# First batch of a fused attention and SoLU layer: P kept in float32 and turned by TensorE, with fewer TensorE turns of z

## The chip, the cores and the metric

One core of a Trainium2 chip runs the whole program. The metric is the device time of one execution in microseconds, as the median over several runs; the kernel before was run three times.

## What is computed

Two parts in a row. Attention with decay over 8 batches of 8 heads, sequence 576, head width 64:

```
scores = q k^T / 8 + (cum_q - cum_k), masked above the diagonal; cum = cumsum(log(clip(f, 1e-4, 1)))
P      = exp(scores - max) / (sum + 1e-9)
attn   = P v
```

Its output, 4608 tokens of 512, goes through one feed-forward layer:

```
h    = x w_in                       (512 -> 1024)
solu = h * softmax(h)
z    = (solu - mean) / sqrt(var + 1e-6) * g_ln
out  = z w_out                      (1024 -> 512)
```

Everything is float32 at the interface. Inside, most products are made from float16 halves: an operand is split into a high and a low half, and three products (high-high, low-high, high-low) stand for one.

## The kernel before, in words

**Attention.** Two heads make a pair, four pairs a batch, 32 pairs (p = 0 to 31) in all. A pair's 576 query rows lie in five tiles (i = 0 to 4): the first has 64 rows, the others 128; tile i needs 64 + 128 i key columns, so a tile's width is 64, 192, 320, 448 or 576. `score_products` makes the scores on TensorE in PSUM (the first 8 pairs in float32, the later ones from float16 halves). `scores` does the rest of the softmax: DVE adds the mask and takes the maximum (L839), ACT takes the exponential and its sum (L844), GpSimd prepares the divisor (L850), DVE inverts it (L851). For tiles 0 and 1 (`HOME`) the exponentials stay in PSUM, for tiles 2 to 4 they go to SBUF (`pt`). Then P is split: a cast to float16 with the division (`copied`, L500 on ACT for tiles 0 to 3, L502 on GpSimd for tile 4; table `P_HI`), and the rest as a low half by DVE (L866). `transposes` turns both halves by a DMA issued on SP (`turned_dma`, L509), one DMA for each tile, 160 in all. `values` multiplies by v, whose halves `split_v` has made (L782 on GpSimd, L783 on DVE): for each tile i there are i + 1 key blocks, 15 a pair, each with three float16 products for each of two heads, which run side by side in two column halves of the array (L888). ACT and DVE split the result into the layer's x (`x_h` L897, `x_l` L898).

**The layer.** 36 blocks of 128 tokens ("layers" 0 to 35 below). 24 products of 512 columns make h (L918 to L920) in one PSUM tile `hps`; DVE takes the maximum (L929), ACT the exponential (L932), DVE the weighted product (L936), ACT the squares (L946), GpSimd the statistics (L940 to L951). Then z is normalised and turned, with 24 products behind it (L988 to L990; the last layer has its own, L1001 to L1004). For layers `TURNED[0]` <= n < `TURNED[1]`, before 3 to 32, z is normalised by GpSimd (L956), split into halves by ACT (L500) and GpSimd (L960), and turned by one DMA. In the other six, GpSimd or DVE normalises z (L965), TensorE turns it (L976, eight turns of 128 columns), and ACT and DVE split it as they take it out of PSUM (L979, L980).

**Weights.** The inputs are stored as pairs of 32-bit words, from which ACT and DVE decode float32 values: ACT one word (L579), then the top bits of the other, either by ACT into PSUM in two halves (L593) with two DVE passes (L599), or, where `W_TOP` says GpSimd, in one pass of 1024 columns in SBUF and one DVE pass. Eight such blocks: four of W_in, four of W_out. ACT sums squares of W_out (L728) for its scale and of v (L680) for theirs.

**Order.** Every piece of work is recorded by `op(engine, ns, due, ...)`. `Plan.schedule` walks through time with the planner's costs `ns` and its own delays, and on each engine takes, of what can start, the piece with the smallest `due`. `due` is not the time given at the call but `RANK[seq]`, a table of some 3,700 numbers. The result is a fixed instruction order on each engine. Six PSUM banks (`ps`) are handed out by the plan. Where the plan leaves TensorE idle in its first 300 us, products of the identity with itself (fillers, L1112, 256 columns) are put into the order:

```
                for _ in range(many):
                    nc.tensor.matmul(dst[:, :256], blank[:, :P], blank, start=True, stop=True)
```

The first half (tiles 0 to 2) of all four pairs of batch 0 comes first, then the second half (tiles 3 and 4); layers 0 and 1 (tokens under 320) need the first half alone.

Of the kernel before, what the change touches and what calls it, by code (L numbers as in the profile page):

```python
# [1156 lines left out]
```

## Time and profile before

| | |
|---|---|
| median of 3 runs | 682.15 us (680.62 to 682.84) |
| profiled execution | 680.34 us, its span 678.6 us |
| TensorE busy | 648.1 us (95% of the span) |
| DVE, ACT, GpSimd busy | 567.1, 528.8, 374.4 us |
[...]

The busy time of TensorE counts fillers as it counts real products, and a product's duration includes its drain, in which the next one already runs; the pace of a run of products is read from the distance of their starts. "Idle before" in a row is the time that the engine stood idle ahead of the group, with what ended it.

### The profile page before, as it was taken

Reading aid. Unit: us, or ns where it says so; the run is one execution under the profiler, and the core shown is the slowest. Engines: PE = TensorE matmul, PEld = TensorE weight load, DVE = VectorE, ACT = ScalarE, POOL = GpSimd, SP = SyncE. Lnnn points to the kernel's source line nnn. Section 1 sums busy time; section 2 is a strip of 40 time slices with the busy share of each in tenths; the row PEclk is TensorE's granted clock in tenths of the full one; section 3 lists DMA queues with packets and bytes.
Section 4 is the critical chain, followed back from the end, with each engine's and each line's share of the span. In section 5 each row is a group of like instructions: output and inputs, shape, how many; then the busy total and the mean of one; then the engine's idle time right before and its main releaser. Section 6 shows DMA issues by size and latency. Waiting matters only on the chain. (4 is left out here: it accounts for less than half of the span.)

```text
span 678.6 us, 17916 instructions
## 1 busy us (share of the span) xinstructions
PE 648.1 (95%) x6573; PEld 355.4 (52%) x6573; DVE 567.1 (84%) x1672; ACT 528.8 (78%) x1320; POOL 374.4 (55%) x591
## 2 busy tenths in 40 slices
PE   6999999999998999999999999998999999899998
PEld 4667555555544445545454545454454555454545
DVE  6796999998997899999899879999999987766232
ACT  6999977799878977979887878978776787665423
POOL 3211364456557845767578746776576854454410
PEclk9999999999999999999999999999999999999999
DMA  8999579989989998999699799898864986487501
GB/s 338 329 237 312 102 126 168 226 167 145 182 135 234 176 196 146 204 201 213 136 219 223 126 199 176 151 192 208 155 118 88 194 136 122 92 156 145 116 1 62
DMA packets 284280, 116.21 MB, mean 171 GB/s; under 512 B 269856, under 2 KB 270304, under 8 KB 283168
## 3 DMA queue, kind: packets, MB, share of 16 engines
q1 hardware_dynamic: 284192, 115.07, 81.8%
q8 instruction: 51, 0.84, 0.5%
q14 instruction: 37, 0.30, 0.2%
HBM read 38.27 MB, written 9.66 MB: 71 GB/s over the span
## 5 line engine op out<-in xcount | busy, mean ns | idle before, releaser
L844 ACT ACTIVATE p<-p,nm 128x448 f32<-128x448 f32 (+2 forms) x192 | 126.9, 662 | 30.1 <-DVE nm L839 27.7
L850 POOL TENSOR_SCALAR sm<-sm 128x2 f32<-128x2 f32 (+1 forms) x128 | 39.6, 309 | 149.6 <-ACT p L844 104.9
L818 PE MATMUL ps<-qk 64*128 64x288 f16 (+9 forms) x1056 | 105.1, 305 | 11.2 <-DVE nm L839 4.2
L918 PE MATMUL hps<-wi_h,x_h 128*128 128x512 f16 x288 | 109.6, 381 | 4.9 <-DVE e L936 4.9
L920 PE MATMUL hps<-wi_h,x_l 128*128 128x512 f16 x288 | 109.1, 379 | 0.0
L919 PE MATMUL hps<-wi_l,x_h 128*128 128x512 f16 x288 | 109.1, 379 | 0.0
L866 DVE SCALAR_TENSOR_TENSOR wo_p<-p,ri,wo_p 128x576 f16<-128x576 f32 (+1 forms) x128 | 104.8, 845 | 3.6 <-POOL wo_p L502 2.1
L988 PE MATMUL ps<-wo_f,zz 128*128 128x512 f16 x280 | 106.7, 381 | 1.0 <-DVE nm L839 0.4
L990 PE MATMUL ps<-wo_f,zz 128*128 128x512 f16 x280 | 106.1, 379 | 0.0
L989 PE MATMUL ps<-wo_f,zz 128*128 128x512 f16 x280 | 106.1, 379 | 0.0
L888 PEld LDWEIGHTS <-v 128*64 128x64 f16 x2880 | 81.6, 110 | 31.8 <-issue 28.0
L888 PE MATMUL ps<-t_p,v 128*64 128x128 f16 (+1 forms) x2880 | 93.4, 219 | 4.4 <-DMA t_p<-p16s 1.3
L839 DVE CUSTOM_DVE_ANT_0 p<-ps,mask 128x448 f32<-128x448 f32 (+2 forms) x192 | 94.2, 513 | 2.9 <-PE ps L816 2.5
L960 POOL TENSOR_TENSOR z<-e,z 128x1024 f16<-128x1024 f32 x30 | 66.7, 2222 | 19.1 <-ACT z L500 18.5
L502 POOL TENSOR_SCALAR wo_p<-p,ri 128x576 f16<-128x576 f32 x64 | 54.7, 862 | 17.8 <-DVE ri L851 13.3
L929 DVE TENSOR_REDUCE st<-hps 128x1 f32<-128x1024 f32 x36 | 43.7, 1215 | 13.7 <-PE hps L920 13.4
L936 DVE SCALAR_TENSOR_TENSOR e<-hps,e 128x1024 f32<-128x1024 f32 x36 | 43.9, 1220 | 12.9 <-ACT e L932 12.8
L818 PEld LDWEIGHTS <-qk 64*128 64x128 f16 x864 | 32.9, 94 | 39.8 <-issue 26.9
L932 ACT ACTIVATE e<-hps,st,unscale 128x1024 f32<-128x1024 f32 x32 | 38.4, 1201 | 19.4 <-DVE st L930 18.1
L816 PE MATMUL ps<-crow,pick 64*128 64x448 bf16 (+1 forms) x360 | 52.4, 276 | 0.0
L866 DVE SCALAR_TENSOR_TENSOR p16s<-ps,ri,p16s 64x64 f16<-64x64 f32 (+1 forms) x128 | 38.9, 338 | 14.2 <-ACT p16s L500 13.9
L500 ACT ACTIVATE wo_p<-p,ri 128x448 f16<-128x448 f32 x64 | 40.0, 660 | 13.7 <-DVE ri L851 8.8
(178 smaller groups left out, 1305.8 us busy)
## 6 DMA issues: line engine op xcount, KB each, us to landing
raws<-in_qk_dram SPq DMA_DIRECT2D x24, 576.0 KB, 5.1
vraw<-in_v_dram SPq DMA_DIRECT2D x8, 1280.0 KB, 7.2
out_dram<-y SPq DMA_DIRECT2D x35, 256.0 KB, 2.8
qk<-in_qk_dram SPq DMA_DIRECT2D x8, 576.0 KB, 7.4
wo_raw<-in_w_in_dram SPq DMA_DIRECT2D x4, 1024.0 KB, 8.6
vraw<-in_w_out_dram SPq DMA_DIRECT2D x2, 1024.0 KB, 5.3
t_raw<-in_w_out_dram SPq DMA_DIRECT2D x2, 1024.0 KB, 6.2
t_p<-p16s SPq DMA_TRANSPOSE x96, 3.6
```

Of the source, the lines that this page charges most:

```text
L818: nc.tensor.matmul(dst, x[row(h), 0, q0:q0 + P], y[row(h), 1, cols], start=(n == 0), stop=False)
L839: op(DVE, R_NS[i] if n == 0 else 442, at[i][h] + STEPS[0], lambda i=i, h=h, n=n, a=a, e=e, x=x, m0=m0: nc.vector.tensor_tensor_reduce(home ...
L844: op(ACT, E_NS[i] + (28 if i in (2, 3) else 0), at[i][h] + STEPS[1], lambda i=i, h=h, x=x: nc.scalar.activation(home(i, h), home(i, h), AF ...
L866: op(DVE, L_NS[j], at[j][g] + STEPS[4], lambda j=j, g=g, nq=nq, h16=h16, l16=l16, r1=r1: nc.vector.scalar_tensor_tensor(l16(), home(j, g, ...
L888: nc.tensor.matmul(o[row(h), a:a + n], v16[m][:, x, 2 * j + h], t[:, y, i + j if h else i - j], start=(j == 0 and c == 0), stop=(j == i an ...
L918: nc.tensor.matmul(hps[:, sl], x_h, wi_h[:, c, sl], start=(c == 0), stop=False)
L919: nc.tensor.matmul(hps[:, sl], x_h, wi_l[:, c, sl], start=False, stop=False)
L920: nc.tensor.matmul(hps[:, sl], x_l, wi_h[:, c, sl], start=False, stop=(c == NCC - 1))
L960: op(Z_LO[n], {DVE: 1280, POOL: 2130}[Z_LO[n]], at, lambda: engine(Z_LO[n]).tensor_tensor(z16[:, :, 1], e2, z16[:, :, 0], ALU.subtract), [ ...
L988: nc.tensor.matmul(o, zz[:, a, 0, j], wo(0, k), start=(k == 0), stop=False)
L989: nc.tensor.matmul(o, zz[:, a, 0, j], wo(1, k), start=False, stop=False)
L990: nc.tensor.matmul(o, zz[:, a, 1, j], wo(0, k), start=False, stop=(k == NFC - 1))
```

## The change

- **P of the first batch** (pairs under `NFP * NPAIR` = 4) is not split. The exponentials of all five tiles go to SBUF (`banked` replaces `HOME`). GpSimd divides them in place, in float32 (`P_SCALE`, 10 instructions a pair). TensorE turns them in blocks of 128 columns, up to four to a PSUM bank (`pieces`; 25 blocks a pair); ACT (tiles 0 to 2) or DVE (tiles 3 and 4) copies them to SBUF (`T_COPY`, 9 copies a pair). The products with v are float32 on the raw v; v's scale moves to the pass that takes x out of PSUM. `split_v` is left out for these pairs.
- **W_out's top bits** are read by GpSimd (`W_TOP`), with one DVE pass instead of two.
- **z of layers 33 and 34** is turned by DMA too (`TURNED`).
- **`RANK`** is another table throughout.

```
+NFP = 1
+P_SCALE, T_COPY = (3, 3, 3, 3, 3), (1, 1, 1, 2, 2)
-W_TOP = (1, 1, 1, 1, 1, 1, 1, 1)
+W_TOP = (1, 1, 1, 1, 3, 3, 3, 3)
-TURNED = (3, 33)
+TURNED = (3, 35)
...
+        if p < NFP * NPAIR:
+            for j, g in each:
+                nq, w = q_n(j), 64 + P * j
+                copied(P_SCALE[j], {POOL: N_NS[j], ACT: 187 + 0.83 * w, DVE: 67 + 0.6 * w}, at[j][g] + STEPS[3], *[lambda j=j, g=g, nq=nq: home(j, g, nq)] * 2,
+                       [("ri", m, j), ("p", j)], [("p", j, g)], scale=ri[m][:nq, j, g:g + 1], by=1.0 / P_UP)
+            return
...
+                def turn(a=a, e=e, key=key):
+                    for s in range(a, e):
+                        nc.tensor.transpose(ps[plan.place[key]][:, (s - a) * nq:(s - a + 1) * nq], pt[i][:nq, s * P:s * P + P], ident[:nq, :nq])
...
+            if exact:
+                t = t.rearrange("p x s w -> p (x s w)").bitcast(F32).rearrange("p (s w) -> p s w", w=n)
+                for j in range(i + 1):
+                    for h in range(2):
+                        nc.tensor.matmul(o[row(h), a:a + n], vraw[b % 2][:, hp, 2 * j + h], t[:, i + j if h else i - j], start=(j == 0), stop=(j == i))
+                return
...
-        split_v(p, at + due["v"] + AT_P[p][1])
+        if p >= NFP * NPAIR:
+            split_v(p, at + due["v"] + AT_P[p][1])
```

How the order moves, at three places. Lines of the changed kernel are shifted: L500 and L502 become L507 and L509, L506 and L509 (DMAs) L513 and L516, L818 becomes L825, L844 L851, L888 L928, L897 L938, L918 L959, L1112 L1154.

ACT, before, up to the first `x_h` of the first batch (`p16s` are the halves of tiles 0 to 2, `p_63` the exponentials of tile 2, `ps` PSUM banks):

```order
L500 ACTIVATE p16s_81<-ps_145,ri_89 128x192
L844 ACTIVATE p_63,sm_93<-p_63,nm_85 128x320 x2
L500 ACTIVATE p16s_81<-ps_145,ri_89 64x64
L500 ACTIVATE p16s_81<-ps_143,ri_89 128x192
L844 ACTIVATE ps_147,sm_94<-ps_147,nm_86 128x64
L500 ACTIVATE p16s_81<-p_63,ri_89 128x320 x2
L844 ACTIVATE ps_146,sm_94<-ps_146,nm_86 128x64
L844 ACTIVATE ps_146,sm_94<-ps_146,nm_86 128x192
L844 ACTIVATE ps_147,sm_94<-ps_147,nm_86 128x192
L500 ACTIVATE p16s_81<-ps_143,ri_89 64x64
L897 ACTIVATE x_h<-ps_145 128x320
```

The same engine in the change, behind its first `x_h` and up to the second (`t_0_p`, `t_1_p` are the turned P):

```order
L938 ACTIVATE x_h<-ps_146,scale_117 128x320
L851 ACTIVATE p_63,sm_95<-p_63,nm_87 128x64
L851 ACTIVATE p_64,sm_95<-p_64,nm_87 128x192
L851 ACTIVATE p_63,sm_95<-p_63,nm_87 128x64
L507 ACTIVATE t_1_p<-ps_148 128x384
L851 ACTIVATE p_64,sm_95<-p_64,nm_87 128x192
L507 ACTIVATE wi_h<-z_104,scale_wi 128x1024
L851 ACTIVATE p_65,sm_95<-p_65,nm_87 128x320 x2
L507 ACTIVATE wi_h<-e_103,scale_wi 128x1024
L938 ACTIVATE x_h<-ps_146,scale_117 128x320
```

The casts of P are gone from ACT, copies of turned P stand between the exponentials, and all exponentials are in SBUF tiles.

TensorE, before, at a short run of fillers between two pairs' products with v:

```order
L888 LDWEIGHTS v_1_78
L888 MATMUL ps_145<-t_1_p,v_1_78 64x128
L1112 LDWEIGHTS ident
L1112 MATMUL hps<-ident 128x256
L1112 LDWEIGHTS ident
L1112 MATMUL hps<-ident 128x256
L888 LDWEIGHTS v_0_77
L888 MATMUL ps_144<-t_0_p,v_0_77 64x64
```

TensorE in the change, just ahead of the first layer's first product (L923 are float32 products with v, L898 turns of P, the float32 weight load being part of the instruction):

```order
L923 MATMUL ps_146<-t_1_p,vraw_76 64x128 x10
L898 MATMUL ps_148<-ident,p_66 128x128 x4
L898 MATMUL ps_150<-ident,p_66 128x128 x3
L1154 LDWEIGHTS ident
L1154 MATMUL ps_145<-ident 128x256
L1154 LDWEIGHTS ident
L1154 MATMUL ps_145<-ident 128x256
L898 MATMUL ps_145<-ident,p_67 128x128 x3
L898 MATMUL ps_146<-ident,p_67 128x128 x3
L959 LDWEIGHTS x_h
L959 MATMUL hps<-wi_h,x_h 128x512
```

In TensorE's whole order there are 363 fillers before and 130 in the change.

SP, the DMA queue, before, behind the loads of the inputs (`c_scratch` and `crow` are the prefix sums on their way through DRAM):

```order
L506 DMA c_scratch<-t_0_cc 32x1728
L509 DMA_TRANSPOSE t_0_p<-p16s_81 128x10x128
L509 DMA_TRANSPOSE t_0_p<-p16s_81 128x2x64
L509 DMA_TRANSPOSE t_0_p<-p16s_81 128x6x128
L509 DMA_TRANSPOSE t_1_p<-p16s_82 128x2x64
L509 DMA_TRANSPOSE t_1_p<-p16s_82 128x6x128
L506 DMA crow<-c_scratch 48x576 x2
L506 DMA c_scratch<-t_0_cc 32x1728
L509 DMA_TRANSPOSE t_1_p<-p16s_82 128x10x128
L506 DMA vraw_75<-in_w_out_dram 128x2048
L506 DMA t_0_raw<-in_w_out_dram 128x2048
```

And in the change:

```order
L513 DMA c_scratch<-t_0_cc 32x1728
L513 DMA crow<-c_scratch 48x576
L513 DMA c_scratch<-t_0_cc 32x1728
L513 DMA crow<-c_scratch 48x576 x3
L513 DMA t_0_raw<-in_w_out_dram 128x2048
L513 DMA vraw_77<-in_w_out_dram 128x2048
L513 DMA qk_0_70<-in_qk_dram 128x1152
L513 DMA t_0_raw<-in_w_out_dram 128x2048
```

The first batch's 20 turning DMAs are gone, and the loads of W_out stand directly behind the prefix sums.

## Rows read from the trace of the kernel before

**Rows 1.** Windows: length; busy us of PE, PEld, DVE, ACT, POOL; granted clock; DMA; GB/s.

```profile
20.00:77.00 57.00, 52.81 (x559) 39.71 (x555) 46.84 (x152) 55.41 (x136) 12.92 (x28) 1.00 0.89 244
100.00:120.00 20.00, 19.66 (x204) 10.74 (x204) 19.59 (x69) 16.25 (x51) 9.88 (x18) 1.00 0.90 164
```

**Rows 2.** Timeline, TensorE, at 77 us: start, us, engine, line, operation.

```profile
77.12 0.39 PE L918 MATMUL hps<-wi_h,x_h 128*128 128x512 f16 x1
```

**Rows 3.** Windows of line L1112 (fillers) alone.

```profile
0.00:77.00 77.00, 44.31 (x346) 33.58 (x346) 0.98 0.88 271
77.00:680.00 603.00, 2.55 (x17) 1.49 (x17) 1.00 0.82 158
```

**Rows 4.** Timeline, TensorE, at 20 us: a run of fillers.

```profile
20.28 3.01 PE L1112 MATMUL hps<-ident 128*128 128x256 bf16 x26
```

**Rows 5.** Timeline, TensorE, at 645 us: four turns of z.

```profile
645.24 0.60 PE L976 MATMUL ps<-ident,z 128*128 128x128 f32 x4
645.68 0.38 PE L988 MATMUL ps<-wo_f,zz 128*128 128x512 f16 x1
```

**Rows 6.** Chain of work that ended last: products with v of a whole pair.

```profile
524.45 2.56 PE ps L888 x90
```

**Rows 7.** Timeline, TensorE, at 18 us: float32 score products of two heads.

```profile
18.48 0.57 PE L818 MATMUL ps<-qk 64*128 64x192 f32 x4
18.89 0.41 PE L814 MATMUL ps<-t_cc,e 64*128 64x192 bf16 x6
19.14 0.80 PE L818 MATMUL ps<-qk 64*128 64x320 f32 x4
19.77 0.44 PE L814 MATMUL ps<-t_cc,e 64*128 64x320 bf16 x4
```

**Rows 8.** Timeline, layer 32's maximum and its turning DMA; then landing times of such DMAs.

```profile
625.16 1.22 DVE L929 TENSOR_REDUCE st<-hps 128x1 f32<-128x1024 f32 x1 [2.61 <-PE hps L920]
636.27 1.93 SPq L509 DMA_TRANSPOSE zz<-z  x1
DMA to landing us min/median/max: 4.2/4.4/6.0
```

**Rows 9.** Groups, ACT: busy us, mean ns of one, idle before and its releasers.

```profile
L500 ACT ACTIVATE wo_p<-p,ri 128x448 f16<-128x448 f32 x64 | 40.0, 660 | 13.7 <-DVE ri L851 8.8 <-issue 4.4 <-POOL unscale_(0, 1)_131 L708 0.5
L500 ACT ACTIVATE p16s<-p,ri 128x320 f16<-128x320 f32 x64 | 33.9, 556 | 3.5 <-DVE ri L851 3.0 <-ACT p L844 0.3
L500 ACT ACTIVATE p16s<-ps,ri 128x192 f16<-128x192 f32 x64 | 25.5, 411 | 2.3 <-DVE ri L851 1.4 <-ACT p L844 0.6
L500 ACT ACTIVATE p16s<-ps,ri 64x64 f16<-64x64 f32 x64 | 18.8, 304 | 0.4 <-DVE p16s L866 0.2
L593 ACT ACTIVATE ps<-t_raw 128x512 int32<-128x512 uint8 x4 | 2.5, 626 | 0.0
```

**Rows 10.** Groups, DVE (the first and last hold two shapes each).

```profile
L866 DVE SCALAR_TENSOR_TENSOR wo_p<-p,ri,wo_p 128x576 f16<-128x576 f32 (+1 forms) x128 | 104.8, 845 | 3.6 <-POOL wo_p L502 2.1
L866 DVE SCALAR_TENSOR_TENSOR p16s<-p,ri,p16s 128x320 f16<-128x320 f32 x64 | 40.8, 658 | 2.8 <-ACT p16s L500 2.5
L980 DVE TENSOR_TENSOR zz<-ps,zz 128x512 f16<-128x512 f32 x12 | 8.1, 682 | 14.8 <-ACT zz L979 14.7
L866 DVE SCALAR_TENSOR_TENSOR p16s<-ps,ri,p16s 64x64 f16<-64x64 f32 (+1 forms) x128 | 38.9, 338 | 14.2 <-ACT p16s L500 13.9
```

**Rows 11.** Groups, GpSimd; the third is from the timeline at 622 us.

```profile
L502 POOL TENSOR_SCALAR wo_p<-p,ri 128x576 f16<-128x576 f32 x64 | 54.7, 862 | 17.8 <-DVE ri L851 13.3 <-DVE wo_f L744 3.2
L956 POOL TENSOR_SCALAR e<-e,st 128x1024 f32<-128x1024 f32 x30 | 43.2, 1441 | 2.7
622.66 0.74 POOL L502 TENSOR_SCALAR wo_p<-p,ri 128x576 f16<-128x576 f32 x1 [0.30 <-DVE ri L851]
```

**Rows 12.** Windows at the first lower clock.

```profile
8.00:14.00 6.00, 1.29 (x17) 0.85 (x16) 5.46 (x10) 5.21 (x10) 0.75 (x2) 0.96 1.00 419
14.00:16.00 2.00, 2.00 (x16) 1.57 (x16) 2.00 (x5) 1.50 (x2) 1.51 (x4) 0.50 1.06 446
```

More of the change, by code (lines that the diff above doesn't have):

```diff
@@ L27, with banked @@
 BIG = 3.0e38
+def banked(p, i):
+    return HOME[i] and p >= NFP * NPAIR
 def q_lo(i):
@@ L408, in buf @@
         return held[tag][1]
-    pt = [None if HOME[i] else sb(f"p_{i}", (2 * i + 1) * P) for i in range(NQ)]
+    pt = [sb(f"p_{i}", (2 * i + 1) * P) for i in range(NQ)]
     mask = sb("mask", S + P, dtype=BF16)
@@ L494, in engine, with copied @@
         return {DVE: nc.vector, POOL: nc.gpsimd}[e]
-    def copied(eng, ns, due, out_, in_, reads, writes, scale=1.0, clear=(), port=True):
+    def copied(eng, ns, due, out_, in_, reads, writes, scale=1.0, clear=(), port=True, by=1.0):
         def fn():
@@ L501, in fn @@
             else:
-                (nc.vector if eng == DVE else nc.gpsimd).tensor_scalar(now(out_), now(in_), scale, 1.0, ALU.mult, ALU.mult)
+                (nc.vector if eng == DVE else nc.gpsimd).tensor_scalar(now(out_), now(in_), scale, by, ALU.mult, ALU.mult)
         op(eng, ns[eng], due, fn, reads, writes, clear=clear, port=port and eng == DVE)
@@ L830, in home @@
             w = 64 + P * i
-            return bank(p, i, h)[:nq, :w] if HOME[i] else pt[i][:nq, h * w:(h + 1) * w]
+            return bank(p, i, h)[:nq, :w] if banked(p, i) else pt[i][:nq, h * w:(h + 1) * w]
         def token(i, h):
-            return ("sb", *score_keys(p, i, h)[0]) if HOME[i] else ("p", i, h)
+            return ("sb", *score_keys(p, i, h)[0]) if banked(p, i) else ("p", i, h)
         for i, h in each:
@@ L840, in scores @@
                     home(i, h)[:, a:e], bank(p, i, h, n)[:, :e - a], mask[:, m0 + a:m0 + e], -0.125 / (QK if p >= NAT * NPAIR else 1.0), x if n else BIG, ALU.add, ALU.min, accum_out=x),
-                   [score_keys(p, i, h)[n], ("mask",)], [token(i, h), ("nm", m, i, h)], clear=[] if HOME[i] else [("p", i)])
+                   [score_keys(p, i, h)[n], ("mask",)], [token(i, h), ("nm", m, i, h)], clear=[] if banked(p, i) else [("p", i)])
         for i, h in each:
             x = nm[m][:, i, h:h + 1]
-            op(ACT, E_NS[i] + (28 if i in (2, 3) else 0), at[i][h] + STEPS[1], lambda i=i, h=h, x=x: nc.scalar.activation(
+            op(ACT, E_NS[i] + (0 if banked(p, i) or i == 4 else 28), at[i][h] + STEPS[1], lambda i=i, h=h, x=x: nc.scalar.activation(
                 home(i, h), home(i, h), AF.Exp, bias=x, scale=-1.0, accum_out=sm[m][:, i, h:h + 1]),
-               [*(score_keys(p, i, h) if HOME[i] else []), ("nm", m, i, h), ("table",)], [token(i, h), ("sm", m, i, h)])
+               [*(score_keys(p, i, h) if banked(p, i) else []), ("nm", m, i, h), ("table",)], [token(i, h), ("sm", m, i, h)])
         i = group[-1]
@@ L855, in scores @@
             h16 = lambda w=w, j=j, g=g, nq=nq: p16(p, j, 0)[:nq, g * w:(g + 1) * w]
-            reads = [("ri", m, j), *score_keys(p, j, g), token(j, g)] if HOME[j] else [("ri", m, j), ("p", j, g), ("p", j)]
-            prior = [("w32", c) for c in (2 * n2, 2 * n2 + 1)] + [("w32", "s", k) for k in range(4 * n2, 4 * n2 + 4)] if p < 2 and j > 2 else []
-            copied(P_HI[j], {POOL: N_NS[j], ACT: (158 if HOME[j] else 187) + 0.83 * w, DVE: 67 + 1.05 * w}, at[j][g] + STEPS[3], h16, lambda j=j, g=g, nq=nq: home(j, g, nq),
-                   reads, [("p16", n2, j, g)], scale=r1, clear=prior, port=not HOME[j])
+            reads = [("ri", m, j), *score_keys(p, j, g), token(j, g)] if banked(p, j) else [("ri", m, j), ("p", j, g), ("p", j)]
+            prior = [("w32", c) for c in (2 * n2, 2 * n2 + 1)] + [("w32", "s", k) for k in range(4 * n2, 4 * n2 + 4)] if p - NFP * NPAIR < 2 and j > 2 else []
+            copied(P_HI[j], {POOL: N_NS[j], ACT: (158 if banked(p, j) else 187) + 0.83 * w, DVE: 67 + 1.05 * w}, at[j][g] + STEPS[3], h16, lambda j=j, g=g, nq=nq: home(j, g, nq),
+                   reads, [("p16", n2, j, g)], scale=r1, clear=prior, port=not banked(p, j))
         for j, g in each:
@@ L863, in scores, with pieces @@
             h16, l16 = (lambda n=n, w=w, j=j, g=g, nq=nq: p16(p, j, n)[:nq, g * w:(g + 1) * w] for n in range(2))
-            reads = [("ri", m, j), *score_keys(p, j, g), token(j, g)] if HOME[j] else [("ri", m, j), ("p", j, g), ("p", j)]
-            prior = [("w32", c) for c in (2 * n2, 2 * n2 + 1)] + [("w32", "s", k) for k in range(4 * n2, 4 * n2 + 4)] if p < 2 and j > 2 else []
+            reads = [("ri", m, j), *score_keys(p, j, g), token(j, g)] if banked(p, j) else [("ri", m, j), ("p", j, g), ("p", j)]
+            prior = [("w32", c) for c in (2 * n2, 2 * n2 + 1)] + [("w32", "s", k) for k in range(4 * n2, 4 * n2 + 4)] if p - NFP * NPAIR < 2 and j > 2 else []
             op(DVE, L_NS[j], at[j][g] + STEPS[4], lambda j=j, g=g, nq=nq, h16=h16, l16=l16, r1=r1: nc.vector.scalar_tensor_tensor(l16(), home(j, g, nq), r1, h16(), ALU.mult, ALU.subtract),
-               [*reads, ("p16", n2, j, g)], [("p16l", n2, j, g)], port=not HOME[j], clear=prior)
+               [*reads, ("p16", n2, j, g)], [("p16l", n2, j, g)], port=not banked(p, j), clear=prior)
+    def pieces(i):
+        n = 2 * i + 1
+        k = -(-n // 4)
+        return [(n * c // k, n * (c + 1) // k) for c in range(k)]
     def transposes(p, i, at):
@@ L871, in transposes @@
         to = [("t1raw",)] if i > 2 and p == 0 else []
+        if p < NFP * NPAIR:
+            t = lambda: turned_p(p, i).rearrange("p x s w -> p (x s w)").bitcast(F32)
+            for c, (a, e) in enumerate(pieces(i)):
+                key = ("s", "pt", p, i, c)
+                def turn(a=a, e=e, key=key):
+                    for s in range(a, e):
+                        nc.tensor.transpose(ps[plan.place[key]][:, (s - a) * nq:(s - a + 1) * nq], pt[i][:nq, s * P:s * P + P], ident[:nq, :nq])
+                op(PE, (e - a) * TRANSPOSE, at + 0.1 * c, turn, [("p", i), ("p", i, 0), ("p", i, 1), ("const",)], [key], take=key, form=TURNS)
+                w = (e - a) * nq
+                copied(T_COPY[i], {ACT: 75 + 0.83 * w, DVE: 72 + 1.05 * w}, at + 0.1 * c + 0.5, lambda a=a, e=e: t()[:, a * nq:e * nq], lambda w=w, key=key: ps[plan.place[key]][:, :w],
+                       [key], [("pt", m * (i < 3), i, c)], clear=[("pt", m * (i < 3), i), *to], port=False)
+            return
         turned_dma(at, lambda: turned_p(p, i).rearrange("p x s w -> p (x s) w"), lambda: p16(p, i)[:nq], nq // 16 * 2 * (2 * i + 1),
@@ L880, in values @@
         tiles = ((0, 1, 2), (3, 4))[half]
+        exact = p < NFP * NPAIR
         def product(i):
@@ L884, in product @@
             a, n = q_lo(i) - 320 * half, q_n(i)
+            if exact:
[3 more added lines that the diff above has]
+                        nc.tensor.matmul(o[row(h), a:a + n], vraw[b % 2][:, hp, 2 * j + h], t[:, i + j if h else i - j], start=(j == 0), stop=(j == i))
+                return
             for j in range(i + 1):
@@ L891, in values @@
         for i in tiles:
-            ns = (6 if i else 3.6) * (i + 1) * 30
-            op(PE, ns, at + 0.2 * (i - tiles[0]), lambda i=i: product(i), [("pt", p % 2 * (i < 3), i), ("v16", m), ("v16l", m)], [key],
+            ns = (6 if i else 3.6) * (i + 1) * (40 if exact else 30)
+            reads = [("vr", b % 2, hp), *(("pt", p % 2 * (i < 3), i, c) for c in range(len(pieces(i))))] if exact else [("v16", m), ("v16l", m)]
+            op(PE, ns, at + 0.2 * (i - tiles[0]), lambda i=i: product(i), [("pt", p % 2 * (i < 3), i), *reads], [key],
                take=key if i == tiles[0] else None, clear=[xk], form=HALVES)
-        up = 1.0 / P_UP
+        up, uk = (scales[b][:, 1, 0:1], [("scale", b, 0)]) if exact else (1.0 / P_UP, [])
         xo = [t[:, hp, x0:x0 + w] for t in x16]
-        op(ACT, 68 + 0.83 * w, at + XSTEP[0], lambda: nc.scalar.activation(xo[0], ps[plan.place[key]][:, :w], AF.Copy, scale=up), [key], [xk])
+        op(ACT, 68 + 0.83 * w, at + XSTEP[0], lambda: nc.scalar.activation(xo[0], ps[plan.place[key]][:, :w], AF.Copy, scale=up), [key, *uk], [xk])
         op(DVE, 72 + 1.05 * w, at + XSTEP[1], lambda: nc.vector.scalar_tensor_tensor(
-            xo[1], ps[plan.place[key]][:, :w], up, xo[0], ALU.mult, ALU.subtract), [key, xk], [(*xk, "l")], clear=[xk])
+            xo[1], ps[plan.place[key]][:, :w], up, xo[0], ALU.mult, ALU.subtract), [key, xk, *uk], [(*xk, "l")], clear=[xk])
     def layer(n, at):
```

290 rows, old and new, of the table RANK are left out of this document.

## The prediction

> **What bounds the kernel now.** I read the windows first. Between 20 and 77 us ACT is busy 55.4 of 57 us, DVE 46.8, GpSimd 12.9; between 100 and 120 us TensorE (19.66 of 20) and DVE (19.59) are the full ones [rows 1]. So there are two stages: a start that ends at 77.12 us, when the first layer's first product runs [rows 2], and a rest that is set by TensorE. TensorE's 52.8 busy us in the start mislead: the windows of line L1112 alone show 346 of its 363 filler products before 77 us and 17 after [rows 3]. A filler computes nothing; 26 in a row take 3.01 us, the last one's drain of 0.27 included, so one is (3.01 - 0.27)/25 = 0.109 us [rows 4] and 346 are 37.8 us. Of the first 77.1 us only 39.3 hold real products and waits. The start is set by ACT, and TensorE is padded while it waits.
>
> **The change part by part, on TensorE's own line.** The fillers are instructions of the program; each costs its time whatever is late, so they belong in the sum. The order of the change holds 130: 111 before the first layer's first product, 19 behind it.
>
> 1. Fillers: 363 - 130 = 233 fewer, 233 x 0.109 = -25.5 us (235 fewer before the first layer, 2 more behind).
> 2. P of the first batch is turned by TensorE: 25 blocks a pair, 100 for four pairs. Four such turns of z take 645.68 - 645.24 = 0.44 us [rows 5], 0.109 each: +10.9 us, 49 of them before the first layer, 51 behind.
> 3. P times v: a pair has 15 steps of two products side by side. Before, a step was three f16 passes: 90 products, 45 passes of two, in 2.56 us [rows 6], 0.057 a pass, 0.171 a step. Now it is one float32 step of 128 columns, which no row shows. The nearest are float32 score products, side by side too: 192 columns took 18.89 - 18.48 = 0.41 us, 320 took 0.63 [rows 7]; on the line through them 128 columns take 0.30, the upper bound. The lower bound is four times the f16 pace, 0.227. Each score product there comes behind other work and its surplus over four passes is about the same at 192 and 320 columns (0.07 and 0.06), as an entry cost; steps in a row should pay it seldom, so I take 0.25. 60 steps x (0.25 - 0.171) = +4.7 us, between +3.4 and +7.7.
> 4. z of layers 33 and 34 goes by DMA: 16 turns fewer, -1.7 us. Their wait: in layer 32 the maximum starts at 625.16, the turning DMA is issued at 636.27 and lands 4.2 to 6.0 us later [rows 8], 15.3 to 17.1 us. Behind layer 34's last input product the order holds 81 products of 512 columns from other layers; at twice a filler's 256 columns, 0.218 us each, they are 17.7 us: covered with little to spare, 0 to +1 us; I take 0.
>
> Sum: -25.5 + 10.9 + 4.7 - 1.7 = -11.6 us, if TensorE's unfilled waits stay as they are. Up to the first layer: -235 x 0.109 + 49 x 0.109 + 24 steps (the three small tiles of four pairs) x 0.079 = -18.4, so the first layer starts near 58.7 us; behind it +6.8 come back (51 turns, 36 steps, 2 fillers, less 1.7).
>
> **Can the engine that sets the start follow?** ACT's rows in front of the fourth x_h, for which the first layer waits, are the test. The order shows what leaves: 24 casts of P at 0.304, 0.411 and 0.556 us (8 of each, 10.2 us) and 2 at 0.660 (1.3); 8 reads of W_out's top bits at 0.626 (5.0) [rows 9]; and, put behind it, 13 wider passes (3 casts, 5 squares and 2 decodings of W_out, 3 squares of v), each of 512 columns or more and so at least the 0.660 of a 448-column cast: 8.6 us or more. What comes: 16 copies out of PSUM, 4 of 64 columns, 4 of 256, 8 of 384. By the casts' rows 64 columns are 0.30 and 384 lie between 0.556 (320) and 0.660 (448), about 0.61; 256 about 0.48: 8.0 us. ACT is relieved by at least 10.2 + 1.3 + 5.0 + 8.6 - 8.0 = 17.1 us, about the 18.4 that TensorE's line asks. The passes put behind meet an ACT that has room at 100 to 120 us (16.25 of 20 [rows 1]).
>
> DVE loses the low halves of P, 4 of 32 pairs of (104.8 + 40.8 + 38.9) us [rows 10], 23.1 us, and four low halves of v, and gains 20 copies of at most 0.68 us (the subtraction of 512 columns out of PSUM in the same rows), 13.6 at most: relieved by 9.5 or more. GpSimd pays: 40 divisions of P. 576 columns took 0.862 us and 1024 took 1.441 [rows 11]; on the line through them 64, 192, 320 and 448 are 0.20, 0.37, 0.53 and 0.70: 2.66 a head, 21.3 us for eight. Add 4 reads of top bits, 1024 columns each, 5.8; take off 8 casts of 576 columns, 6.9. Some 20 us more on an engine with 44 idle in the 57 us: covered by number, late by turn, since each division now stands between DVE's reciprocal and TensorE's turn. What is late next is therefore GpSimd. The DMA queue loses 20 turning DMAs of P, each queued on SP among loads, a relief; W_out's loads then follow those of the prefix sums at once.
>
> [...]
>
> The sum stands against the profiled execution: 680.34 - 11.6 = 668.7 us. The median of the runs shown, 682.15, is 1.8 above that execution, so I predict **670.5 us** for a median.
>
> **Rivals.**
> [...]
> - *The waits shrink too.* SP's queue and DVE are relieved. DVE is full from 100 us on and sheds 9.5 us or more; if 5 to 12 us of TensorE's waits behind 77 us go with it: 658 to 665.
> [...]
> - *The start's gain is eaten later* (no change). If DVE, not TensorE, sets the time from 100 us on, an earlier first layer only waits there: 680 to 684. Against: DVE's own relief is nearly as large as the gain.
>
> **How the numbers follow.** About 0.3%, 2 us, can be told from no change. Forecast, 665 to 676 (the bounds of step 3 and 3 us of waits either way): 0.62. GpSimd paces: 0.13, all but the edge of it faster. Waits shrink: 0.12. Clock: 0.07. Eaten later: 0.06. Faster 0.87, same 0.06, slower 0.07. The range 661 to 678 takes in the forecast, nearly all of the GpSimd case and half of the shrinking waits, about 0.8.
>
> **What would show it.** In the profile after: 130 fillers with 111 before the first layer; the first layer's first product at 57 to 61 us (77.12); turns of P at 0.109 each; float32 steps at 0.23 to 0.30; GpSimd's divisions at 0.3 to 0.9 us and 30 to 36 of its first 60 us busy; granted clock 1.00 from 20 us on; the time from the first layer's first product to the end near 608 us against 601.5. I am wrong if the first layer starts after 66 us (GpSimd or the clock), or if it starts near 59 and the rest takes over 615 us (something later takes the gain back).

## The result, and the profile after

| | before | after |
|---|---|---|
| median of the runs | 682.50 us (4 runs, 680.62 to 683.39) | 665.66 us (4 runs, 663.76 to 667.03) |
| ratio | | 0.9757, 95% interval 0.9729 to 0.9785 |
| span of the profiled execution | 678.6 us | 661.9 us (run of 663.76 us) |
| first layer's first product | 77.12 us [rows 2] | 55.41 us |
| from there to the end of the span | 601.5 us | 606.5 us |

The change is faster by 16.8 us. A second set of runs (the last experiment below) gave 666.10 us and 0.9782 (0.9765 to 0.9799). The start is 21.7 us shorter, and 5.0 us of it are given back behind it.

The page of the kernel after, its busy times:

```profile
PE 633.3 (96%) x6304; PEld 343.2 (52%) x6304; DVE 558.0 (84%) x1640; ACT 519.7 (79%) x1294; POOL 403.0 (61%) x625
```

Its windows up to the first layer and at 100 us (columns as in [rows 1]):

```profile
0.00:55.40 55.40, 44.72 (x406) 31.07 (x407) 37.97 (x122) 47.30 (x116) 28.72 (x74) 0.97 0.76 285
20.00:55.40 35.40, 31.19 (x315) 21.23 (x316) 24.23 (x88) 33.65 (x92) 22.07 (x45) 1.00 0.69 250
100.00:120.00 20.00, 19.87 (x182) 10.82 (x182) 19.27 (x76) 18.11 (x47) 2.93 (x7) 1.00 0.92 228
```

The same window of the kernel before, up to its first layer:

```profile
0.00:77.10 77.10, 66.49 (x658) 49.30 (x658) 60.65 (x182) 69.23 (x160) 19.52 (x57) 0.98 0.88 271
```

The fourth busy column is ACT: 69.23 of 77.1 us before, 47.30 of 55.4 after. ACT's work ahead of the first layer fell by 21.9 us, the start by 21.7, and ACT's idle time in it stayed (7.9 and 8.1 us). That is the gain, in two parts. The first layer needs the fourth `x_h` of ACT, which comes at 73.36 us before and 53.83 after; the windows up to there:

```profile
0.00:73.36 73.36, 63.85 (x637) 47.61 (x638) 56.91 (x173) 65.49 (x154) 17.30 (x53) 0.98 0.92 282
0.00:53.83 53.83, 43.15 (x392) 29.53 (x393) 36.96 (x118) 45.73 (x114) 27.52 (x73) 0.97 0.77 286
```

So ACT's rows ahead of it fell by 19.8 us, and it comes 19.5 us earlier. The other 2.2 us lie between this `x_h` and the first product: 3.76 us before, in which TensorE waits for DVE and then makes two scores ahead of the layer, and 1.58 after.

```profile
75.70 0.76 PE L818 MATMUL ps<-qk 64*128 64x288 f32 x4 [1.10 <-DVE x_l L898]
```

TensorE of the kernel after, the windows of the fillers alone (L1154), against [rows 3]; 111 and 19 of them:

```profile
0.00:55.40 55.40, 17.69 (x111) 11.59 (x111) 0.97 0.76 285
55.40:662.00 606.60, 2.57 (x19) 1.77 (x19) 1.00 0.78 157
```

Its timeline on TensorE, at the first layer and at a tile of five float32 steps, against [rows 2, 5, 6]:

```profile
54.75 0.82 PE L898 MATMUL ps<-ident,p 128*128 128x128 f32 x6
55.41 0.38 PE L959 MATMUL hps<-wi_h,x_h 128*128 128x512 f16 x1
...
107.40 1.31 PE L923 MATMUL ps<-t_p,vraw 128*64 128x128 f32 x20
```

Six turns take 0.82 us with the last one's drain of 0.27: 0.110 each. The 20 records are five steps of two products with two records each: (1.31 - 0.27)/19 x 4 = 0.219 us a step.

### The profile page after: what moved, and what is told of

It is laid out like the page before. It is cut to its first block, busy times and chain, and to the rows that moved or that the text cites. A ratio compares the mean times of both kernels' runs of the same rounds, so it can differ in the third digit from the quotient of the medians.

```text
span 661.9 us, 17333 instructions
## 1 busy us (share of the span) xinstructions
PE 633.3 (96%) x6304; PEld 343.2 (52%) x6304; DVE 558.0 (84%) x1640; ACT 519.7 (79%) x1294; POOL 403.0 (61%) x625
## 3 DMA queue, kind: packets, MB, share of 16 engines
q1 hardware_dynamic: 262624, 109.69, 77.1%
## 5 line engine op out<-in xcount | busy, mean ns | idle before, releaser
L851 ACT ACTIVATE p<-p,nm 128x448 f32<-128x448 f32 (+4 forms) x208 | 132.9, 641 | 25.7 <-DVE nm L846 25.3
L825 PE MATMUL ps<-qk 64*128 64x288 f16 (+9 forms) x1056 | 103.3, 306 | 8.6 <-DMA qk<-in_qk_dram 4.9
L959 PE MATMUL hps<-wi_h,x_h 128*128 128x512 f16 x288 | 109.6, 381 | 1.8 <-DVE e L977 1.8
L846 DVE CUSTOM_DVE_ANT_0 p<-ps,mask 128x448 f32<-128x448 f32 (+4 forms) x208 | 97.6, 497 | 5.8 <-PE ps L823 3.0
L879 DVE SCALAR_TENSOR_TENSOR wo_p<-p,ri,wo_p 128x448 f16<-128x448 f32 (+1 forms) x112 | 96.5, 880 | 3.7 <-ACT wo_p L507 2.6
L1001 POOL TENSOR_TENSOR z<-e,z 128x1024 f16<-128x1024 f32 x32 | 71.6, 2239 | 21.6 <-ACT z L507 21.2
L928 PE MATMUL ps<-t_p,v 128*64 128x128 f16 (+1 forms) x2520 | 80.7, 219 | 3.1 <-DVE nm L846 1.5
L928 PEld LDWEIGHTS <-v 128*64 128x64 f16 x2520 | 70.8, 110 | 24.7 <-issue 22.6
L509 POOL TENSOR_SCALAR wo_p<-p,ri 128x576 f16<-128x576 f32 x56 | 52.9, 952 | 14.9 <-DVE ri L858 10.1
L825 PEld LDWEIGHTS <-qk 64*128 64x128 f16 x864 | 32.3, 94 | 37.0 <-issue 26.1
L997 POOL TENSOR_SCALAR e<-e,st 128x1024 f32<-128x1024 f32 x32 | 47.4, 1483 | 2.9
L509 POOL TENSOR_SCALAR qk<-raws,scale 128x576 f16<-128x576 f32 x48 | 40.3, 844 | 14.6 <-DVE scale L676 8.3
```

The lines of the kernel that those rows point to most:

```text
L509: (nc.vector if eng == DVE else nc.gpsimd).tensor_scalar(now(out_), now(in_), scale, by, ALU.mult, ALU.mult)
L825: nc.tensor.matmul(dst, x[row(h), 0, q0:q0 + P], y[row(h), 1, cols], start=(n == 0), stop=False)
L846: op(DVE, R_NS[i] if n == 0 else 442, at[i][h] + STEPS[0], lambda i=i, h=h, n=n, a=a, e=e, x=x, m0=m0: nc.vector.tensor_tensor_reduce(home ...
L851: op(ACT, E_NS[i] + (0 if banked(p, i) or i == 4 else 28), at[i][h] + STEPS[1], lambda i=i, h=h, x=x: nc.scalar.activation(home(i, h), hom ...
L879: op(DVE, L_NS[j], at[j][g] + STEPS[4], lambda j=j, g=g, nq=nq, h16=h16, l16=l16, r1=r1: nc.vector.scalar_tensor_tensor(l16(), home(j, g, ...
L928: nc.tensor.matmul(o[row(h), a:a + n], v16[m][:, x, 2 * j + h], t[:, y, i + j if h else i - j], start=(j == 0 and c == 0), stop=(j == i an ...
```

## The experiments

Those of one group are told together. "Start" is the time of the first layer's first product. In most of them the order of every engine is the changed kernel's, and only the engine that does a piece, or what it does, is another.

### Are the fillers the cause? e1 and e2

The same edit in the kernel before (e1) and in the changed kernel (e2); what is left out computes nothing:

```
-                for _ in range(many):
+                for _ in range(0):
```

> The kernel before without its 363 fillers, everything else in the same order. If ACT sets the start and the fillers only pad TensorE there, the first layer's first product stays at 76 to 78 us (77.12 with them) and the time within 2 us of 682: fewer fillers are then a sign of a shorter start and not its cause. If a filler costs its time (346 x 0.109 = 37.8 us ahead of the first layer), the first layer starts 15 to 38 us earlier and the time falls by as much, past the changed kernel. If the fillers hold the clock up, windows up to 77 us show a granted clock near 0.5 and the time rises by 5 us or more.

> The changed kernel without its 130 fillers, everything else in the same order. If the start is set by ACT and the clock stays up on the real work alone, the first layer's first product stays at 54 to 57 us (55.4 with them), the granted clock at 1.00 from 20 us on, and the time is 0 to 2 us shorter (19 fillers behind the first layer are 2.1 us). If 130 is already about as few as the clock bears, windows between 20 and 60 us show a clock below 0.9 and the time rises by 5 to 25 us.

e1, its window from 20 us to the first layer:

```profile
20.00:81.30 61.30, 35.52 (x268) 21.62 (x263) 48.57 (x154) 56.48 (x139) 13.03 (x28) 0.57 0.83 231
```

Its first layer's first two products on the timeline:

```profile
81.30 0.61 PE L918 MATMUL hps<-wi_h,x_h 128*128 128x512 f16 x1
81.70 0.63 PE L919 MATMUL hps<-wi_l,x_h 128*128 128x512 f16 x1
```

e2, three windows:

```profile
20.00:60.00 40.00, 33.91 (x274) 22.96 (x274) 26.31 (x91) 35.80 (x97) 24.31 (x46) 0.79 0.60 220
20.00:40.00 20.00, 18.36 (x154) 12.89 (x155) 12.12 (x50) 17.29 (x50) 8.96 (x24) 0.66 0.53 201
120.00:140.00 20.00, 17.21 (x171) 9.52 (x171) 18.50 (x72) 17.96 (x49) 9.68 (x17) 0.91 0.92 153
```

Its first layer's first product:

```profile
57.97 0.38 PE L959 MATMUL hps<-wi_h,x_h 128*128 128x512 f16 x1
```

e1: 683.00 us, ratio 1.0028 (1.0012 to 1.0044). All 363 fillers are gone, 39.6 us of TensorE's instructions, and nothing is gained: waits stand in their place, and the start is 4.2 us later. The granted clock is 0.57 on average between 20 and 81 us (1.00 from 20 to 77 with the fillers), 0.50 from 60 to 80, and the layer's first two products start 0.40 us apart, where the kernel before has 0.22 (77.12 and 77.34 us). e2: 669.47 us, ratio 0.9823 (0.9789 to 0.9857); the start is 2.6 us later with a clock of 0.66 from 20 to 40 us, the clock is at 0.91 once more from 120 to 140 us, and the time is 3 to 4 us above the changed kernel's. So fewer fillers are a sign of a shorter start and no cause: without fillers in either kernel the change is still worth 13.5 us (683.00 to 669.47). What the fillers are worth by these two runs is about 2 us in the kernel before and 3 to 4 in the changed one, both less than the 5 us or more that the expectations put on a lower clock.

### Is it ACT, or GpSimd? e3, e10, e4 and e6

e3 puts the 40 divisions of P on ACT (and leaves `P_UP` out of the divisor, so that x stays as it was); e10 lets ACT read W_out's top bits:

```
-  copied(P_SCALE[j], ...)
+  op(POOL, N_NS[j], ..., lambda x=x, r1=r1: nc.scalar.activation(x(), x(), AF.Copy, scale=r1), ...)
...
-  op(POOL, 1150, due, lambda: nc.gpsimd.tensor_scalar(words(0), ..., 1 / 32, -31 / 64, ALU.mult, ALU.add), ...)
+  op(POOL, 1150, due, lambda: nc.scalar.activation(words(0), ..., AF.Copy, scale=1 / 32, bias=-31 / 64), ...)
```

e4 divides and multiplies once more; e6 does unrelated work behind each pair's last small division:

```
+  nc.gpsimd.tensor_scalar(x(), x(), 1.0, 1.0, ALU.mult, ALU.mult)
...
+                def divide(x=x, r1=r1, more=14 if (j, g) == (0, 1) else 0):
...
+                    for _ in range(more):
+                        nc.gpsimd.tensor_scalar(spare, spare, 1.0, 1.0, ALU.mult, ALU.mult)
```

> The changed kernel with the 40 divisions of the first batch's P on ACT in place of GpSimd, at the same places of the order. ACT is busy 38.1 of the 40 us from 20 to 60 us; 24 divisions ahead of the first layer cost it 8 x (0.304 + 0.411 + 0.556) = 10.2 us by the casts' rows of the kernel before. If ACT sets the start, the first layer's first product moves from 55.4 to 63 to 67 us and the time rises by 7 to 12 us over the changed kernel. If GpSimd paces the start, its 13 us of divisions there go, the first layer starts at 55 us or earlier and the time is the same or shorter.

> The changed kernel with the top bits of W_out read by ACT in place of GpSimd, in the same one pass of 1024 columns and at the same places of the order (the rest of that part of the change stays). Three of the four passes stand ahead of the first layer; at 1.15 us each, as ACT's decodings of 1024 columns take, they are 3.5 us. If ACT sets the start, the first layer starts at 57.5 to 60 us (55.4) and the time is 2 to 5 us longer. If GpSimd does, it is relieved of as much, the first layer starts at 52 to 55 us and the time is the same or shorter.

> The changed kernel with a second multiplication by 1.0, in place, behind each of GpSimd's 40 divisions of P: the work of one more division, 8 x (0.657 + 0.428 + 0.534) = 13.0 us ahead of the first layer and 12.3 behind it. If GpSimd has room (24.1 of the 40 us from 20 to 60 us are busy), each pair's chain gets 1 to 3 us longer, the first layer starts at 55 to 59 us (55.4) and the time rises by 0 to 3 us. If GpSimd paces the start, the first layer starts near 68 us and the time rises by 10 us or more.

> The changed kernel with 14 extra GpSimd multiplications of 128x64 in a buffer that nobody reads, behind the last division of each pair's small tiles: by the 0.24 us of a 64x64 one 3.3 us a pair and 13 us ahead of the first layer, as many as the second multiplication brought, but behind the chain and not in it. If GpSimd's idle time there is room (1.6, 2.1 and 2.3 us stand idle behind the divisions of the first three pairs), the first layer starts at 56 to 60 us (55.4) and the time rises by 1 to 5 us. If GpSimd's total work sets the start, it is as with the second multiplication: near 68 us, and 13 us or more longer.

Windows up to the first layer. Of e3:

```profile
0.00:64.80 64.80, 48.08 (x406) 32.98 (x407) 37.84 (x120) 57.45 (x144) 13.67 (x47) 0.89 0.64 244
```

Of e10:

```profile
0.00:56.60 56.60, 45.16 (x407) 31.05 (x408) 38.29 (x122) 49.23 (x119) 25.14 (x71) 0.94 0.73 275
```

Of e4:

```profile
0.00:67.80 67.80, 49.61 (x407) 34.00 (x408) 38.63 (x122) 48.09 (x117) 39.48 (x102) 0.90 0.62 233
```

Of e6:

```profile
0.00:69.00 69.00, 48.80 (x407) 33.09 (x408) 38.87 (x123) 48.70 (x119) 45.01 (x131) 0.89 0.61 229
```

e3: 680.03 us, ratio 0.9983 (0.9964 to 1.0003). ACT has 10.2 us more to do ahead of the first layer, as the casts' rows said, and the start is 9.4 us later. Behind it 5 us more are lost, more than expected. A likely reason, not tested by itself, is that the other 16 divisions meet an ACT that the changed kernel already keeps full (19.87 of 20 us from 60 to 80). e10: 668.09 us, ratio 0.9821 (0.9797 to 0.9845); two passes of 1.14 us, not three, came ahead of the first layer; ACT does 1.9 us more, the start is 1.2 us later. ACT's idle time is 7.4 us in both (7.9 and 8.1 in the two kernels). So far ACT's sum goes with the start.

e4 and e6 contradict that it does so alone. e4: 682.98 us, ratio 1.0022 (1.0001 to 1.0042); GpSimd does 10.8 us more (39.48 for 28.72) and the start is 12.4 us later, although GpSimd stood idle in 27 of the 55 us. e6: 679.64 us, ratio 0.9980 (0.9964 to 0.9997). The extra work, in a buffer that nobody waits for, was longer than meant:

```profile
L870 POOL TENSOR_SCALAR spare<-spare 128x64 f32<-128x64 f32 x56 | 15.5, 276 | 4.6
```

With the 4.6 us between them that is 20.1 us of GpSimd's turn, and the start is 13.6 us later: by this run GpSimd had some 6 us to spare. All four blocks count, since turns of the first pair's tile 3 stand ahead of the first layer on TensorE and wait for GpSimd behind the fourth. The clock is lower too, in e4 and e6 alike (20 to 60 us, 1.00 in the changed kernel):

```profile
20.00:60.00 40.00, 29.69 (x263) 19.58 (x263) 22.34 (x83) 30.22 (x84) 26.11 (x63) 0.91 0.53 196
20.00:60.00 40.00, 30.12 (x272) 19.41 (x269) 23.07 (x83) 30.29 (x84) 31.00 (x82) 0.91 0.51 184
```

A part of the 12.4 and 13.6 us can be this clock's, but not most of them: in e2 it was 0.79 in the same window, and the start was 2.6 us later. Who waited for whom in e4, on ACT from 12 us to the first layer (us in total, times, longest):

```profile
ACT t_p L507 <- PE ps L902: 9.6, 5, 2.4
```

The same in the changed kernel, on GpSimd from 20 us to the first layer:

```profile
POOL sm L857 <- ACT p L851: 12.2, 7, 4.9
```

It is a round: GpSimd waits for ACT's exponentials, TensorE's turns wait for GpSimd's divisions, ACT's copies wait for the turns, and ACT, which does all in a fixed order, holds the next pair's exponentials behind them. GpSimd's idle time is for the most part that wait for its turn, and not room. The waits show each link; that together they make the 12 to 14 us is the reading that fits both runs.

### Can the start be shortened further? e5, e9 and e11

The small tiles' divisions (e5) and tile 2's copies out of PSUM (e9) go to DVE, and so do W_in's top bits (e11):

```
+  (nc.gpsimd if j > 2 else nc.vector).tensor_scalar(x(), x(), r1, 1.0 / P_UP, ALU.mult, ALU.mult)
...
-            if eng == ACT:
+            if eng == ACT and not by_dve:
...
-  nc.scalar.activation(bits(), ..., AF.Copy, scale=1 / 32, bias=-31 / 64)
+  nc.vector.tensor_scalar(bits(), words(0)[:, sl], 29, None, ALU.logical_shift_right)
```

> The changed kernel with the 24 divisions of the small tiles (0 to 2) on DVE in place of GpSimd, at the same places of the order; tiles 3 and 4 stay on GpSimd. If the start is a chain through ACT, GpSimd, DVE, TensorE and ACT, whose steps add up although no engine but ACT is full, each division that takes less than GpSimd's 0.313, 0.428 and 0.534 us shortens it, and the hop from DVE's reciprocal to GpSimd goes: the first layer's first product at 50 to 54 us (55.4) and the time 2 to 5 us below the changed kernel's. If DVE's own order is what is tight (28.8 of the 40 us from 20 to 60 us are busy), its maxima wait behind the divisions, the first layer starts at 56 to 60 us and the time is 1 to 5 us longer.

> The changed kernel with the 8 copies of turned P of tile 2 out of PSUM on DVE in place of ACT, at the same places of the order. ACT is busy 47.3 of the 55.4 us up to the first layer and idle only 1.6 us behind 11.6 us; 8 copies at 0.481 us are 3.8 us of it. If ACT sets the start, the first layer's first product comes at 51.5 to 54 us (55.4) and the time is 1 to 4 us below the changed kernel's. If the chain through GpSimd and DVE is as tight, 8 x 0.548 = 4.4 us on DVE in their turn take it back: first layer at 55 to 58 us, the time the same or up to 3 us longer.

> The changed kernel with the top bits of W_in, 8 reads of 512 columns between 9 and 29 us, on DVE in place of ACT, at the same places of the order. ACT stands idle 1.6 us only between 11.6 us and the first layer, and 7 of the reads, 0.614 us each, lie there: 4.3 us. If ACT alone sets the start from then on, the first layer's first product comes at 51 to 53.5 us (55.4) and the time is 2 to 4 us below the changed kernel's. If DVE, busy 38.0 of these 55.4 us, is behind in its own order, 8 x 0.6 us more there take it back: 54.5 to 57 us, the time within 2 us of the changed kernel's.

Windows up to the first layer. Of e5:

```profile
0.00:55.30 55.30, 46.14 (x407) 31.52 (x408) 43.97 (x146) 47.56 (x116) 16.39 (x50) 0.94 0.74 280
```

Of e9:

```profile
0.00:57.10 57.10, 46.30 (x406) 31.82 (x407) 40.93 (x130) 44.85 (x108) 28.17 (x74) 0.94 0.73 273
```

Of e11:

```profile
0.00:59.30 59.30, 45.02 (x406) 31.40 (x407) 42.04 (x128) 43.27 (x108) 28.62 (x74) 0.91 0.70 267
```

What ACT waited for in e9, from 24 us to the first layer:

```profile
ACT t_p L507 <- PE ps L898: 3.3, 2, 2.5
```

In the changed kernel, from 12 us, it was

```profile
ACT t_p L507 <- PE ps L898: 1.3, 2, 0.8
```

and in e11, from 12 us:

```profile
ACT p L851 <- DVE nm L846: 3.5, 4, 1.3
ACT t_p L507 <- PE ps L898: 2.9, 2, 2.0
```

All three were expected to shorten the start if ACT alone, or the sum of the round's steps, set it, and none does. e5 takes 12.3 us off GpSimd: start 55.3 us, 667.45 us, ratio 0.9781 (0.9760 to 0.9803), no change. e9 takes 2.5 us off ACT: start 57.1 us, 667.97 us, ratio 0.9805 (0.9790 to 0.9820). e11 takes 4.0 us off ACT: start 59.3 us, 668.18 us, ratio 0.9811 (0.9794 to 0.9828). In e9 and e11 ACT waits longer than in the changed kernel, for turns (3.3 and 2.9 us for 1.3) and in e11 for the maximum of DVE, which it did not wait for before. So in no run does the start come earlier than ACT's sum plus some 7.4 us; both kernels, e3, e5 and e10 lie within 0.8 us of that, and where a piece stands in another engine's turn, the start is later. That this sum is a limit is read from these runs and not shown by one that tries to pass it. No experiment points to a faster version in this order.

### The small parts, and the measure: e7, e8 and e12

e7 is the kernel before with two tables changed; the pieces of each table that are new get places in the order of before. e8 takes the second table's change out of the changed kernel. e12 is the changed kernel itself.

```
-W_TOP = (1, 1, 1, 1, 1, 1, 1, 1)
+W_TOP = (1, 1, 1, 1, 3, 3, 3, 3)
-TURNED = (3, 33)
+TURNED = (3, 35)
```

> The kernel before with the two small parts of the change, W_out's top bits by GpSimd and z of layers 33 and 34 turned by DMA, in the order of before with the 12 new pieces put in between. If P is the cause of the gain, ACT sheds 8 reads of 0.626 us, 5.0 us, in the start and the first layer's first product comes at 70 to 75 us (77.12); the time is 676 to 683 us. If the small parts or they above all bring the gain, it is below 670.

> The changed kernel with z of layers 33 and 34 turned by TensorE again, as in the kernel before: 16 turns, +1.7 us on TensorE. If that wait was covered as counted, the first layer is as in the changed kernel (55.4 us) and the time 0 to 3 us longer. If the end of the kernel carries several us of the gain, 4 us or more longer; if the DMA in the end part was waited for, shorter.

> The changed kernel once more, unaltered, as the measure for the experiments whose ratio lies a few tenths of a per cent above its own (0.9757, from 0.9729 to 0.9785): those with small-tile divisions or copies on DVE, top bits on ACT or DVE, and z turned by TensorE (0.978 to 0.982). If these differences are of the experiments, it comes again to 0.974 to 0.978 and its first layer starts at 55 to 56 us. If they are the spread from one set of runs to the next, it comes to 0.979 to 0.981, and all of them but the one with the top bits on DVE count as no change.

The first layer's first product on the timeline of e7:

```profile
73.88 0.38 PE L926 MATMUL hps<-wi_h,x_h 128*128 128x512 f16 x1
```

Of e8:

```profile
56.31 0.38 PE L967 MATMUL hps<-wi_h,x_h 128*128 128x512 f16 x1
```

Of e12:

```profile
55.50 0.38 PE L959 MATMUL hps<-wi_h,x_h 128*128 128x512 f16 x1
```

e7: 682.05 us, ratio 1.0006 (0.9991 to 1.0020). The start is 3.2 us shorter, and the time is not. Its window from the first layer's first input product to its first output product is

```profile
73.90:101.60 27.70, 27.63 (x262) 16.28 (x260) 26.56 (x79) 18.43 (x40) 12.92 (x28) 1.00 0.69 126
```

27.7 us, where the kernel before takes 20.5 (77.1 to 97.6 us): TensorE looks full there, but a part of that is padding. The fillers alone in this window, then in that of the kernel before, and their longest run in e7:

```profile
73.90:101.60 27.70, 5.15 (x43) 3.76 (x41) 1.00 0.69 126
77.10:97.60 20.50, 1.12 (x9) 0.77 (x9) 1.00 0.79 154
83.57 4.10 PE L1120 MATMUL ps<-ident 128*128 128x256 bf16 x36
```

Fillers take 4.0 of the 7.2 us that are longer, since the plan expected TensorE idle where it put them; DVE is busy in 26.56 of the 27.7 us. Whether the 3.2 us are lost to these fillers or to DVE's queue was not tried. The small parts alone, in an order that was not made for them, bring nothing; the gain needs P's part, or the order that was made with it. P's part alone was not tried, because its order would have to be made anew; so what the new order is worth by itself stays open.

e8: 669.04 us, ratio 0.9810 (0.9786 to 0.9833). Beside e12 (666.10 us, 0.9782, 0.9765 to 0.9799) it is 1.9 us slower by the ratios, against 1.7 counted for 16 turns; the intervals overlap. e12 also sets the measure: e5 is the same as the changed kernel, e9, e10 and e11 lie 0.2 to 0.4% above it, with intervals that overlap its own: none is shown to be faster, and none to be slower. Its start is 55.50 us and its span 663.6: the 1.7 us more than in the first profile come behind the first layer.

## Why the prediction was right, and which steps were not

The time of 665.66 us lies in the range (661 to 678) and at the fast end of the forecast case (665 to 676); 670.5 was 4.8 us too slow. Against the profiled execution:

| term | predicted | measured |
|---|---|---|
| fillers | -25.5 | -25.4 (233 x 0.109) |
| turns of P | +10.9 | +11.0 (100 x 0.110) |
| float32 steps | +4.7 (+3.4 to +7.7) | +2.9 (60 x (0.219 - 0.171)) |
| turns of z | -1.7 | -1.8 (16 x 0.110) |
| TensorE's waits | 0 | -3.4; -1.7 in the second profile |
| sum | -11.6 | -16.7; -15.0 |

The waits are what the other terms leave of the spans (678.6 to 661.9 and 663.6).

- **Right: the stage and its engine.** The start goes with ACT [rows 1]; e3 shows it by putting ACT's work back. The forecast fillers are there, 111 and 19. The start came at 55.4, not 58.7 us. The step that was mis-sized is ACT's relief in front of the fourth `x_h`, put at 17.1 us or more, where the windows show 19.8: it took 13 wide passes at the bound of 0.660 us each, and in the kernel before they are longer:

```profile
L680 ACT ACTIVATE junk<-vraw 128x1280 bf16<-128x1280 f32 x5 | 6.3, 1260 | 0.0
L728 ACT ACTIVATE junk<-wo_f,gs 128x512 bf16<-128x512 f32 x8 | 5.7, 713 | 0.1
...
L500 ACT ACTIVATE wo_f<-wo_f,sg 128x512 f16<-128x512 f32 x4 | 2.7, 708 | 0.0
L579 ACT ACTIVATE wo_f<-vraw 128x1024 f32<-128x1024 f32 x2 | 2.3, 1138 | 0.7 <-DMA vraw<-in_w_out_dram 0.7
```

3 x 1.260 + 5 x 0.713 + 3 x 0.708 + 2 x 1.138 = 11.7 us in place of 8.6. The copies of turned P came to 6.2 us in place of 8.0 in the kernel after (its groups on ACT up to the first layer):

```profile
L507 ACT ACTIVATE t_p<-ps 128x384 f32<-128x384 f32 x8 | 3.8, 481 | 0.1
...
L507 ACT ACTIVATE t_p<-ps 128x256 f32<-128x256 f32 x4 | 1.5, 375 | 0.0
...
L507 ACT ACTIVATE t_p<-ps 128x64 f32<-128x64 f32 x4 | 0.9, 216 | 1.3 <-PE ps L898 1.3
```

That makes 17.1 + 3.1 + 1.8 = 22.0. It is more than the 19.8: the exponentials of 64 and 192 columns and the `x_h` themselves became longer (0.342, 0.444 and 0.522 us for 0.278, 0.386 and 0.419; 1.4 us together), and a row's duration overlaps the next one's by some 0.1 us (in the kernel after a square at 51.57 us takes 0.72, and the next instruction starts at 52.18), so that fewer rows save a little less than their sum. The 2.2 us between the fourth `x_h` and the first product were in no step of the prediction.

- **Wrong as a cause: "each costs its time whatever is late, so they belong in the sum".** e1 takes all of them out and gains nothing. The sum came out because the plan puts fillers where it sees TensorE idle, so their number measures how much of the start is padding; TensorE's line was book-keeping, and ACT's line was the argument. That the two came out alike in the prediction (18.4 and 17.1) is luck: both fell short of the 21.7.
- **Wrong as a reason: "an engine with 44 idle in the 57 us: covered by number".** GpSimd did not pace the start, the case that was given 0.13 (55.4 us, and not after 66), but not for that reason: e6 shows about 6 us to spare behind the chain, and e4 none in it. "What is late next is therefore GpSimd" was right. GpSimd was busy for 30.7 of its first 60 us, forecast 30 to 36.
- **Too high: the float32 step.** 0.219 us lies under the lower bound of 0.227: the pace of [rows 6] held a whole pair with its changes from tile to tile, which a run inside one tile has not (30 f16 products inside one tile of the kernel before, the row below: four passes of two take (1.03 - 0.27)/29 x 8 = 0.210 there), and the surplus read from [rows 7], where each product comes behind other work, did not appear in a run of steps.

```profile
69.72 1.03 PE L888 MATMUL ps<-t_p,v 128*64 128x128 f16 x30
```

- **Right: z of layers 33 and 34.** Covered; the window of the kernel after in which the last turning DMAs are under way shows TensorE full:

```profile
612.00:655.00 43.00, 43.00 (x258) 21.45 (x257) 11.97 (x19) 16.95 (x27) 16.16 (x26) 1.00 0.35 74
```

- **The clock** was 1.00 from 20 us on, as forecast. No run shows it making the change slower, the case that was given 0.07: without any filler, at 0.57 from 20 to 81 us (e1) and 0.79 from 20 to 60 (e2), the times are 2 to 4 us longer.
- **Waits shrink, start eaten later.** Behind the first layer 606.5 and 608.1 us were taken, 608 forecast. The first of the two profiles shows 1.7 us of smaller waits that the second does not, so two profiles can't tell how much of them belongs to the change.
- **GpSimd's divisions.** See the last section. The 21.3 us for the 40 divisions came out by luck: undisturbed, the small ones took more than the line by columns says (0.313 us for 0.20) and the large ones less (0.747 for 0.862), 21.3 in all; six longer ones brought 3.9 on top, 25.2.

## What to carry to other kernels

An engine's idle time in a chain whose order is fixed is not room: before work is moved to it, see for whom it waits there, and whether the one that it waits for waits for it in turn. Padding that a planner puts into idle time says how long a stage is; take the gain from the engine that the stage waits for, add up its rows ahead of the stage's end, and use each row's own duration where the trace has it. Where an engine looks full, count the padding in it first. A mean that lies over the quiet value (0.862 us for 0.74 in [rows 11]) can come from a few long ones: look at the median and the longest before a surplus is put on each.
